# Starting the second stage of a two-stage kernel inside the first: normalized h transposed by DMA, weights loaded into freed buffers, and the first spatial block summed while z2 grows

## The chip, the cores and the metric

The kernel runs on one core of a Trainium2 chip. The metric is the time of one execution in device microseconds (us). Most executions of one kernel agree within 0.3%; medians of several runs are quoted. The trace of one profiled execution has a span that is about 2 us shorter than its timed run. A core has five engines with instruction streams of their own: PE (matrix multiply), ACT (activation functions), DVE (elementwise work and statistics), POOL and SP; SP issues the DMAs here. In the traces an engine works through its stream in the order in which it was written, and the streams wait for each other through semaphores.

## The reference, cut to what matters

```python
# stage one: attention over 64 segments of 32 rows, each with 8 memory rows from the segment before
h  = x + A_ref(layernorm(x), mem0, Wq, Wk, Wv, Wo)
# stage two: a gated unit with a mixing matrix over the sequence
def B_ref(x, w_in, w_sp, b_sp, w_out):
    z  = gelu(x @ w_in)                      # 2048 x 1792
    z1 = z[:, :896]
    z2 = layernorm(z[:, 896:])
    g  = w_sp @ z2 + b_sp[:, None]           # 2048 x 2048 times 2048 x 896: the "mixing"
    return (z1 * g) @ w_out
h2 = h + B_ref(layernorm(h), w_in, w_sp, b_sp, w_out)
```

Stage one is serial from segment to segment. Stage two needs h; a row block is 128 of the 2048 rows, so there are 16. The mixing needs all of z2, but a sum over its row blocks may start with the first. The mixing is done in four blocks of 512 outputs; the title and the recorded texts call such a block a spatial block.

## The kernel before: the parts that matter

The code runs through a helper that records each operation with what it reads and writes, and inserts the waits. `pe`, `act`, `dve`, `pool` and `sp` append to an engine's stream, so the order in the text is the order on each engine. Eight PSUM banks take the results of PE.

The end of stage one, and the loads of stage two (cut):

```python
    lastA = em.by_eng["pe"][-1]
    for qr in range(4):
        WoX_mm(RB - 1, qr)            # the last row block's leftover output projection
    WoX_evac(RB - 1)
    WoX_scatter(RB - 1, WXB)
    h_done(RB - 1, WXB)               # adds it to h, statistics of h, stores h to DRAM
    ...
    sp(lambda e: e.dma_start(w_in, winr), writes=["w_in"], after=[lastA])
    for rb in range(RB):
        sp(lambda e, rb=rb: e.dma_start(h_sb[:, rb, :], h_d[rb]), ..., after=[lastA])   # h is read back
    ...                               # w_out, bias
    load_wT(0)                        # w_sp, transposed earlier
    load_wT(1)
```

The loop over row blocks of z2, and the mixing:

```python
    for rb in range(2):
        xn_apply(rb); xT(rb % 2, 6 + rb % 2); xn_copy(rb, 6 + rb % 2)
    for rb in range(RB):
        if rb + 2 < RB:
            xn_apply(rb + 2)                     # DVE: normalize h of block rb+2
        z2_mm(rb, 0)                             # PE: 4 matmuls, then gelu on ACT
        if rb + 2 < RB:
            xT(rb % 2, 6 + rb % 2)               # PE: 4 transposes of block rb+2 into a bank
            xn_copy(rb + 2, 6 + rb % 2)          # DVE: bank to SBUF
        z2_mm(rb, 1)                             # PE: 4 matmuls, then gelu on ACT
        z2_norm(rb)                              # DVE: statistics of z2, wait for both gelus
        if rb > 0:
            z2_apply(rb - 1)                     # DVE: normalize z2
        if rb % 4 == 3:
            for fb in range(FB):
                z1_group(rb // 4, fb)            # PE: 7 groups of 4 matmuls, gelu on ACT
    z2_apply(RB - 1)
    check()                                      # overflow check: DVE, one tiny matmul, DVE
    for tb in range(NTB):                        # 4 blocks of 512 outputs
        for fb in range(FB):
            bank = fb % 2
            for sc in range(RB):                 # 16 mixing matmuls into one bank
                pe(... ps[:, bank, 0:TB], lhsT=z2[:, sc, ...], rhs=wTb[tb % 2][:, :, sc, :] ...)
            ...                                  # "gate": DVE adds the bias, multiplies by z1
            if pend and fb >= 1:
                out_rb(pend.pop(0))              # 7 output matmuls, adds h, stores
```

Of the kernel before, what the change touches and what calls it, by code (L numbers as in the profile page):

```python
# [6 lines left out]
BF = mybir.dt.bfloat16  # L7
# [153 lines left out]
def fast_path(nc, st, keep, A_x, A_mem0, A_Wq, A_Wk, A_Wv, A_Wo, A_seg_len, B_w_in, B_w_sp, B_b_sp, B_w_out, out):  # L161
# [15 lines left out]
    CK = 16  # L177
# [44 lines left out]
    hbuf = sb("hbuf", [128, 4, 512], BF)  # L222
    wst = sb("wst", [128, RB, 64], BF)
# [21 lines left out]
    vext_d = nc.dram_tensor("vext_d", [NCK, 16, 128, 2 * DH], BF, kind="Internal").ap()  # L245
    h_d = nc.dram_tensor("h_d", [RB, 128, D], BF, kind="Internal").ap()
# [396 lines left out]


# [82 lines left out]

    qx_copy(0)
    for s in range(NSEG):
# [17 lines left out]
        for b in range(2):  # L747
            for mi in range(2):
                QK(s, b, mi)
                QK_evac(s, b, mi)  # L750
        S_half(s, 0)
# [5 lines left out]
        S_half(s, 1)  # L757
        sm_exp(1)
        sm_rcp(0)
# [4 lines left out]
        V_half(s, 1, (2, 3))  # L764
        V_evac(1, "act")
        sm_norm(0)
        sm_norm(1)
        if s + 1 < NSEG:
            qx_copy(s + 1)
        ev = gx.pour(16)  # L770
# [25 lines left out]
        mem_out(s)  # L796
# [6 lines left out]
        if j4 == 3:  # L803
            F_group(rb, XB)
            F_add(rb, XB)
        if j4 == 3 and rb >= 1:
            WoX_scatter(rb - 1, WXB)
            h_done(rb - 1, WXB)
    assert not gx.atoms and not gv.atoms
    lastA = em.by_eng["pe"][-1]  # L810
    for qr in range(4):
        WoX_mm(RB - 1, qr)
    WoX_evac(RB - 1)
    WoX_scatter(RB - 1, WXB)
    h_done(RB - 1, WXB)
    endA = em.by_eng["pe"][-1]


    w_in = region(4 * WSZ, DC * F).rearrange("p (dc f) -> p dc f", dc=DC)
    xn2T = region(4 * WSZ + QX, DC * S).rearrange("p (dc t) -> p dc t", dc=DC)  # L820
    h_sb = region(0, RB * D).rearrange("p (rb d) -> p rb d", rb=RB)
    wTb = [region(RB * D, RB * 512).rearrange("p (t sc c) -> p t sc c", sc=RB, c=64),
           region(WSZ, RB * 512).rearrange("p (t sc c) -> p t sc c", sc=RB, c=64)]
    off = WSZ + RB * 512
    w_out = region(off, FB * D).rearrange("p (fb d) -> p fb d", fb=FB)
    off += FB * D
    bsp_b = region(off, S)
    off += S
    gt = region(off, 2 * 2 * 512).bitcast(F32).rearrange("p (j t) -> p j t", j=2)
    off += 2048  # L830
    assert off <= 2 * WSZ
    z2 = region(2 * WSZ, RB * FH).rearrange("p (rb f) -> p rb f", rb=RB)
    z1T = region(3 * WSZ, FB * S).rearrange("p (fb t) -> p fb t", fb=FB)
    TB = 512
    NTB = S // TB
    HF = FH // 2

    winr = B_w_in.rearrange("(dc p) f -> p dc f", p=128)
    sp(lambda e: e.dma_start(w_in, winr), writes=["w_in"], after=[lastA])
    for rb in range(RB):  # L840
        sp(lambda e, rb=rb: e.dma_start(h_sb[:, rb, :], h_d[rb]), reads=[("hd", rb)], writes=[("hs", rb)], after=[lastA])
    woutr = B_w_out.rearrange("(fb p) d -> p fb d", p=128)
    sp(lambda e: e.dma_start(w_out, woutr), writes=["w_out"], after=[lastA])
    sp(lambda e: e.dma_start(bsp_b, bass.AP(B_b_sp.tensor, B_b_sp.offset, [[0, 128], [1, S]])), writes=["bsp"], after=[lastA])
    em.mark_const("w_in", "w_out")

    def load_wT(tb):
        for t in range(8):
            sp(lambda e, t=t: e.dma_start(wTb[tb % 2][:, t, :, :], wT_d[8 * tb + t]), reads=[("wTd", 8 * tb + t)],
               writes=[("wT", tb % 2, t)], after=[lastA])  # L850

    load_wT(0)
    load_wT(1)


# [9 lines left out]
    def xn_apply(rb):  # L865
# [52 lines left out]
    for rb in range(2):  # L918
        xn_apply(rb)
        xT(rb % 2, 6 + rb % 2)  # L920
        xn_copy(rb, 6 + rb % 2)
# [814 lines left out]
```

## Time and profile before

The median is 1034.83 us (3 runs, 1034.33 to 1035.91); the span of the profiled run is 1032.3 us.

| part of the span | from, us | to, us | what PE does |
|---|---|---|---|
| stage one | 0 | 815.55 | to its last output-projection (Wo) matmul |
| hand-over | 815.55 | 832.57 | some 3 us of leftover matmuls that both kernels need, some small ones, waits |
| z2 loop | 832.57 | 902.93 | z2, z1 and transposes |
| mixing and output | 902.93 | 1032.3 | nearly full |

From the page of the profile, part 1 (busy us, share of the span, instructions by engine) and part 4 (the chain that ended last, by engine; PEld are PE's weight loads, SPq and ACTq the queues of SP and ACT, "issue" is time in which an engine waited for nothing that the profile shows):

```profile
PE 899.6 (87%) x18986; PEld 443.2 (43%) x18997; DVE 471.5 (46%) x1059; ACT 489.8 (47%) x1095; POOL 108.0 (10%) x276
PE 79%; ACT 12%; DVE 3%; SPq 2%; issue 2%; DMA 2%; POOL 0%; ACTq 0%
```

PE is the engine to win time on, and it is busy for 87% of the span. The timeline of PE at the hand-over (start, length, engine, line, operation, count; in brackets the idle time before it and what ended it; the first line holds the last Wo matmuls, and two small groups at 816.26 and 816.37 are left out):

```profile
813.64 1.91 PE L579 MATMUL f_ps<-f_arena,f_cT 128*32 128x512 bf16 x32
817.34 0.40 PE L631 MATMUL f_ps<-f_partx,f_Sc 128*32 128x512 bf16 x4 [0.58 <-ACT f_partx L626]
818.53 1.91 PE L621 MATMUL f_ps<-f_arena,f_cTx 128*32 128x512 bf16 x32 [0.80 <-DVE f_hbuf L611]
821.14 0.40 PE L631 MATMUL f_ps<-f_partx,f_Sc 128*32 128x512 bf16 x4 [0.70 <-ACT f_partx L626]
830.72 0.61 PE L346 MATMUL f_ps<-f_ident,f_xn 128*128 128x128 bf16 x4 [9.18 <-DVE f_xn L867]
832.17 0.61 PE L346 MATMUL f_ps<-f_ident,f_xn 128*128 128x128 bf16 x4 [0.84 <-DVE f_xn L867]
832.57 1.70 PE L878 MATMUL f_ps<-f_arena 128*128 128x448 bf16 x4
```

Leftover groups with waits between them, then 9.18 us of idle until the first block of h has come back and been normalized on DVE (the waits list gives that DVE operation 7.0 us of waiting for the DMA of h). The same four transposes take 0.61 us here and 0.40 us later: PE is on a slow clock. The windows view (here 831 to 838 us) gives the clock that PE was granted, after the busy times of the five engines:

```profile
831.00:838.00 7.00, 5.42 (x24) 2.51 (x21) 3.57 (x9) 1.63 (x3) 0.23 (x1) 0.59 1.11 354
```

0.59 of full speed. The Trainium skill, "TensorE: Matmul & The Clock Gate", Part 1, says that PE falls to half rate after an idle window of about 3.4 us and needs about as long of work to recover; the 9.18 us of idle and the 0.59 agree. Finer windows show a granted clock of 0.50 from 823.0 to 836.7 us: it fell 1.5 us after PE's last matmul, and came back 6.0 us after the first transposes.

The chain of waits inside the z2 loop (start, length, what):

```profile
852.98 0.77 PE f_ps L878 x4
853.75 0.02 issue
853.77 0.55 ACT f_arena L881
854.33 0.02 issue
854.35 0.64 DVE f_st L892
854.99 0.02 issue
855.01 0.21 DVE f_mv L894
855.22 0.38 DVE f_arena L903
855.60 0.34 DVE f_xn L867
855.93 0.05 issue
855.98 0.40 PE f_ps L346 x4
856.38 0.77 PE f_ps L878 x4
```

L878 is a z2 group, L881 its gelu, L892 and L894 the statistics of z2, L903 the normalization of the z2 block before, L867 the normalization of h for a later row block, L346 the transposes of that. One turn, from 852.98 to 856.38, is 3.40 us. L867 stands behind L892 in DVE's stream, and PE cannot pass the transposes that wait for L867. In all, PE waits 24.1 us for L867 before twelve groups of transposes.

### The profile page before, as it was taken

Reading aid. Unit: us, or ns where it says so; the run is one execution under the profiler, and the core shown is the slowest. Engines: PE = TensorE matmul, PEld = TensorE weight load, DVE = VectorE, ACT = ScalarE, POOL = GpSimd, SP = SyncE. Lnnn points to the kernel's source line nnn. Section 1 sums busy time; section 2 is a strip of 40 time slices with the busy share of each in tenths; the row PEclk is TensorE's granted clock in tenths of the full one; section 3 lists DMA queues with packets and bytes.
Section 4 is the critical chain, followed back from the end, with each engine's and each line's share of the span. In section 5 each row is a group of like instructions: output and inputs, shape, how many; then the busy total and the mean of one; then the engine's idle time right before and its main releaser. Section 6 shows DMA issues by size and latency. Waiting matters only on the chain.

```text
span 1032.3 us, 41294 instructions
## 1 busy us (share of the span) xinstructions
PE 899.6 (87%) x18986; PEld 443.2 (43%) x18997; DVE 471.5 (46%) x1059; ACT 489.8 (47%) x1095; POOL 108.0 (10%) x276
## 2 busy tenths in 40 slices
PE   5588999999999999899999998888888667899997
PEld 4444444444444444444444444333333223344443
DVE  2144455454455455454544444443444345533443
ACT  2155555665556555555655555655555434500000
POOL 4000001111001111010101000111000012200000
PEclk9889999999999999999999999999999979999999
DMA  9931122121121112112211112020201190002200
GB/s 334 353 73 34 46 45 54 49 57 44 34 49 34 49 39 55 36 47 45 60 48 37 46 44 64 8 65 8 62 13 45 32 352 1 1 8 96 97 16 32
DMA packets 93491, 67.34 MB, mean 65 GB/s; under 512 B 54392, under 2 KB 78336, under 8 KB 93312
## 3 DMA queue, kind: packets, MB, share of 16 engines
q1 hardware_dynamic: 93312, 64.65, 21.4%
q8 instruction: 150, 2.46, 1.0%
q14 instruction: 29, 0.24, 0.1%
HBM read 39.46 MB, written 16.78 MB: 54 GB/s over the span
## 4 chain that ended last, share of the span: by engine, by line
PE 79%; ACT 12%; DVE 3%; SPq 2%; issue 2%; DMA 2%; POOL 0%; ACTq 0%
PE f_ps L436 22%; PE f_ps L579 12%; PE f_ps L956 9%; PE f_ps L530 7%; PE f_ps L380 6%; PE f_ps L621 3%; ACT f_part L591 3%; PE f_ps L496 3%; ACT f_E_sb L489 3%; ACT f_R_sb L508 2%; PE f_ps L911 2%; PE f_ps L944 2%; PE f_ps L547 2%; PE f_ps L597 2%; PE f_ps L878 2%
## 5 line engine op out<-in xcount | busy, mean ns | idle before, releaser
L436 PE MATMUL f_ps<-f_arena,f_hT 128*32 128x512 bf16 x4096 | 233.4, 380 | 15.7 <-ACT f_hT L600 15.6
L443 ACT ACTIVATE f_Tst<-f_ps 128x512 bf16<-128x512 f32 x256 | 152.9, 597 | 112.9 <-PE f_ps L436 112.9
L436 PEld LDWEIGHTS f_ps<-f_arena,f_hT 128*32 128x32 bf16 x4096 | 105.2, 97 | 120.7 <-ACT f_hT L600 20.5
L530 PE MATMUL f_ps<-f_arena,f_hT 128*32 128x512 bf16 x2048 | 143.6, 378 | 0.0
L449 DVE STREAM_TRANSPOSE f_QT<-f_Tst 128x256 uint32<-128x256 uint32 x128 | 56.5, 442 | 188.0 <-ACT f_Tst L443 188.0
L579 PE MATMUL f_ps<-f_arena,f_cT 128*32 128x512 bf16 x2048 | 122.3, 380 | 2.2 <-ACT f_cT L566 2.2
L956 PE MATMUL f_ps<-f_arena 128*128 128x512 bf16 x448 | 99.3, 379 | 3.0 <-DVE f_arena L961 2.4
L591 ACT ACTIVATE f_part<-f_ps 128x512 bf16<-128x512 f32 x64 | 38.2, 597 | 108.0 <-PE f_ps L579 108.0
L452 DVE STREAM_TRANSPOSE f_KT<-f_Tst 128x256 uint32<-128x256 uint32 x128 | 57.0, 445 | 53.1 <-ACT f_Tst L443 53.1
L579 PEld LDWEIGHTS f_ps<-f_arena,f_cT 128*32 128x32 bf16 x2048 | 48.8, 96 | 74.0 <-ACT f_cT L566 32.3
L568 DVE TENSOR_SCALAR f_cT<-f_ps 128x320 bf16<-128x320 f32 x128 | 56.9, 487 | 33.0 <-PE f_ps L553 33.0
L459 POOL COPY f_QT<-f_arena 128x256 bf16<-128x256 bf16 x64 | 29.9, 467 | 397.9 <-PE f_ps L481 397.8
L380 PEld LDWEIGHTS f_ps<-f_hTe,f_arena 128*128 128x128 bf16 x1024 | 61.5, 102 | 20.7 <-issue 20.6
L380 PE MATMUL f_ps<-f_hTe,f_arena 128*128 128x128 bf16 x1024 | 70.1, 227 | 0.0
L956 PEld LDWEIGHTS f_ps<-f_arena 128*128 128x128 bf16 x448 | 43.5, 98 | 56.4 <-DVE f_arena L961 3.8
L516 DVE SCALAR_TENSOR_TENSOR f_E_sb<-f_R_sb,f_E_sb 128x160 bf16<-128x160 f32 x128 | 41.7, 326 | 54.6 <-ACT f_R_sb L512 54.6
L566 ACT ACTIVATE f_cT<-f_ps 128x320 bf16<-128x320 f32 x128 | 49.0, 434 | 37.1 <-PE f_ps L553 37.1
L489 ACT ACTIVATE f_E_sb<-f_ps,f_shift 128x224 bf16<-128x224 f32 x128 | 57.0, 445 | 0.0
L512 ACT ACTIVATE f_R_sb<-f_R_sb,f_rbias 128x160 f32<-128x160 f32 x128 | 54.0, 422 | 2.1
L508 ACT ACTIVATE f_R_sb<-f_ps 128x160 f32<-128x160 f32 x128 | 39.0, 304 | 29.8 <-PE f_ps L501 25.0
L961 DVE TENSOR_TENSOR f_arena<-f_ps,f_arena 128x512 f32<-128x512 f32 x28 | 19.4, 692 | 70.6 <-PE f_ps L956 70.6
L346 PE MATMUL f_ps<-f_ident,f_xn 128*128 128x128 bf16 x144 | 15.8, 238 | 39.3 <-DVE f_xn L867 24.1
(95 smaller groups left out, 1087.3 us busy)
## 6 DMA issues: line engine op xcount, KB each, us to landing
wT_d<-f_wst SPq DMA_DIRECT2D x32, 256.0 KB, 2.3
f_arena<-wT_d SPq DMA_DIRECT2D x32, 256.0 KB, 7.6
f_arena<-in_A_Wq_dram SPq DMA_DIRECT2D x4, 1024.0 KB, 10.5
f_arena<-in_A_Wk_dram SPq DMA_DIRECT2D x4, 1024.0 KB, 14.0
f_arena<-in_A_Wv_dram SPq DMA_DIRECT2D x4, 1024.0 KB, 13.1
f_arena<-in_A_Wo_dram SPq DMA_DIRECT2D x4, 1024.0 KB, 13.9
vext_d<-f_Vs SPq DMA_DIRECT2D x32, 128.0 KB, 2.0
f_Vx<-vext_d SPq DMA_DIRECT2D x64, 64.0 KB, 2.6
```

The source lines that it names most:

```text
L380: pe(lambda e, h=h, dc=dc, hh=hh: e.matmul(ps[:, bank, hh * 128:(hh + 1) * 128], lhsT=ws[:, dc, h * DH:(h + 1) * DH], rhs=hTe[:, ck % 2, d ...
L436: pe(lambda e, dc=dc, c=c, rhs=rhs: e.matmul(ps[32 * c:32 * c + 32, bank, :], lhsT=hT[:, sl, dc, :], rhs=rhs, start=(dc == 0), stop=(dc == ...
L443: act(lambda e: e.activation(out=Tst[:, tb, :].rearrange("p (hp i r) -> p hp i r", i=32, r=2), in_=ps[:, bank, :].rearrange("p (hp r i) -> ...
L449: dve(lambda e: e.transpose(out=dst, in_=src), reads=[("T", tb)], writes=[("QT", b)])
L452: dve(lambda e: e.transpose(out=dst, in_=src), reads=[("T", tb)], writes=[("KT", b)])
L489: act(lambda e: e.activation(out=E_sb[:, b, :], in_=ps[:, bank, 0:224], func=ACT.Exp, scale=scale, bias=shift_sb[:, 0:1]), reads=[PB(bank) ...
L508: act(lambda e: e.activation(out=R_sb[:, b, :], in_=ps[:, bank, 224:384], func=ACT.Ln, scale=LNS), reads=[PB(bank)], writes=[("R", b)])
L530: pe(lambda e, dc=dc, c=c, c0=c0: e.matmul(ps[32 * c:32 * c + 32, bank, :], lhsT=hT[:, sl, dc, :], rhs=w_v[:, dc, c0:c0 + 512], start=(dc ...
L568: dve(lambda e: e.tensor_scalar(out=dst, in0=src, scalar1=UNSC, scalar2=None, op0=ALU.mult), reads=[PB(PVB[c])], writes=[("cT", c)])
L579: pe(lambda e, h=h, g=g, i=i, k=k, b=b: e.matmul(ps[32 * g:32 * g + 32, OB, :], lhsT=cTh[:, i, 8:40], rhs=w_o[:, h, :], start=(first and k ...
L591: act(lambda e: e.activation(out=part[:, s % 4, :], in_=ps[:, OB, :], func=ACT.Copy), reads=[PB(OB)], writes=[("part", s % 4)])
L956: pe(lambda e, fb=fb, sc=sc, bank=bank, tb=tb: e.matmul(ps[:, bank, 0:TB], lhsT=z2[:, sc, fb * 128:(fb + 1) * 128], rhs=wTb[tb % 2][:, :, ...
```

## The change: its intent and its diff

The intent is to start stage two before stage one has ended, and to leave PE no waits in the z2 loop:

1. h is normalized on DVE inside stage one (`xn2_apply`), stored, and transposed by DMA into the freed half of a buffer; only the last two of 16 row blocks are still transposed on PE.
2. w_in, the first w_sp block and the bias are loaded into freed buffers before stage one ends. The first z2 group stands directly behind the last Wo matmul; the leftover projection follows it.
3. z1 groups go two at a time between the row blocks of z2, and the mixing of the first block of outputs, for five of seven column groups in five banks of their own, runs along four row blocks behind z2. z2 and z1 then take turns in three banks, where they had two each.

The diff also leaves out the memory rows of the last segment, which no segment reads (16 small matmuls, L597 of the kernel before).

The diff, cut to its core:

```diff
+    def xn2_apply(rb, j):
+        dve(lambda e: e.tensor_scalar(out=xo[:, j, :], in0=hbuf[:, rb % 4, :], scalar1=mv[:, rb, 0:1], ...
+    def xn2T_dma(rb, after):
+        sp(lambda e: e.dma_start_transpose(out=xts[rb // 8][:, rb % 8, :, :], in_=xn2_d[rb]), ...
 ...                                      # in the loop over the 64 segments of stage one:
+        if s == NSEG - 1:
+            load_wT(0, [lastop["q"]])
 ...
+        if s == NSEG - 1:
+            sp(... w_in1 ..., after=[lastop["s"], lastop["x"]])
+            sp(... bsp_b ..., after=[lastop["k"]])
+            for r in range(8, RB - 2):
+                xn2T_dma(r, [lastop["s"], lastop["x"]])
 ...
+        if j4 == 0 and rb >= 2:
+            xn2_apply(rb - 2, rb % 2)
+            xn2_store(rb - 2, rb % 2)
+        if s == 3 * CK:
+            sp(... w_in2 ..., after=free0)
+        if 0 <= s - 3 * CK - 1 < 8:
+            xn2T_dma(s - 3 * CK - 1, free0)
 ...                                      # stage two:
+    LAG = 4
     for rb in range(RB):
-        if rb + 2 < RB:
-            xn_apply(rb + 2)
-        z2_mm(rb, 0)
-        if rb + 2 < RB:
-            xT(rb % 2, 6 + rb % 2)
-            xn_copy(rb + 2, 6 + rb % 2)
-        z2_mm(rb, 1)
+        z2_mm(rb, 0, zbank())             # three banks in turn for z2 and z1
+        if rb == 0:
+            ...                           # leftovers of row blocks 14 and 15
+        z2_mm(rb, 1, zbank())
+        if rb == 0:
+            for qr in range(4):
+                WoX_mm(RB - 1, qr)
+        ...                               # leftovers, PE transposes of blocks 14 and 15
         z2_norm(rb)
         if rb > 0:
             z2_apply(rb - 1)
-        if rb % 4 == 3:
-            for fb in range(FB):
-                z1_group(rb // 4, fb)
+        for _ in range(2):
+            if rb >= 1 and z1list and (z1list[0][0] < 3 or rb >= 12):
+                tb, fb = z1list.pop(0)
+                z1_group(tb, fb, zbank())
+        if rb >= LAG:
+            for fb, bk in enumerate(ACC):
+                mix(0, fb, rb - LAG, bk)
     z2_apply(RB - 1)
-    check()
 ...                                      # rest of the first block's mixing, then, after that block:
+        if tb == 0:
+            check()
```

More of the change, by code (lines that the diff above doesn't have):

```diff
@@ L222, in fast_path @@
     hbuf = sb("hbuf", [128, 4, 512], BF)
+    xo = sb("xo", [128, 2, 512], BF)
     wst = sb("wst", [128, RB, 64], BF)
@@ L245, in fast_path @@
     vext_d = nc.dram_tensor("vext_d", [NCK, 16, 128, 2 * DH], BF, kind="Internal").ap()
+    xn2_d = nc.dram_tensor("xn2_d", [RB, 128, D], BF, kind="Internal").ap()
     h_d = nc.dram_tensor("h_d", [RB, 128, D], BF, kind="Internal").ap()
@@ L642, in h_done, with xn2_store @@
         sp(lambda e: e.dma_start(h_d[rb], hbuf[:, rb % 4, :]), reads=[("h", rb % 4)], writes=[("hd", rb)])
+    def xn2_apply(rb, j):
+        dve(lambda e: e.tensor_scalar(out=xo[:, j, :], in0=hbuf[:, rb % 4, :], scalar1=mv[:, rb, 0:1], scalar2=rstd[:, rb:rb + 1],
+                                      op0=ALU.subtract, op1=ALU.mult),
+            reads=[("h", rb % 4), ("mv", rb), ("rstd", rb)], writes=[("xo", j)])
+    def xn2_store(rb, j):
+        sp(lambda e: e.dma_start(xn2_d[rb], xo[:, j, :]), reads=[("xo", j)], writes=[("xn2d", rb)])
+    WH = DC * FH
+    w_in2 = region(4 * WSZ, WH).rearrange("p (dc f) -> p dc f", dc=DC)
+    w_in1 = region(4 * WSZ + QX, WH).rearrange("p (dc f) -> p dc f", dc=DC)
+    xts = [region(4 * WSZ + i * QX + WH, 8 * D).rearrange("p (r dc t) -> p r dc t", r=8, dc=DC) for i in range(2)]
+    winr = B_w_in.rearrange("(dc p) f -> p dc f", p=128)
+    def xn2T_dma(rb, after):
+        sp(lambda e: e.dma_start_transpose(out=xts[rb // 8][:, rb % 8, :, :], in_=xn2_d[rb]), reads=[("xn2d", rb)], writes=[("xn2T", rb)],
+           after=after)
     NWT = S // 64
@@ L726, in fast_path, with load_wT @@
     VXN = [2] * 12 + [4, 4, 0, 0]
+    wTb = [region(0, RB * 512).rearrange("p (t sc c) -> p t sc c", sc=RB, c=64),
+           region(3 * WSZ, RB * 512).rearrange("p (t sc c) -> p t sc c", sc=RB, c=64)]
+    h_sb = region(RB * 512, RB * D).rearrange("p (rb d) -> p rb d", rb=RB)
+    z1T = region(WSZ, FB * S).rearrange("p (fb t) -> p fb t", fb=FB)
+    bsp_b = region(WSZ + FB * S, S)
+    z2 = region(2 * WSZ, RB * FH).rearrange("p (rb f) -> p rb f", rb=RB)
+    gt = region(2 * WSZ + RB * FH, 2048).bitcast(F32).rearrange("p (j t) -> p j t", j=2)
+    w_out = region(3 * WSZ + RB * 512, FB * D).rearrange("p (fb d) -> p fb d", fb=FB)
+    def load_wT(tb, after):
+        for t in range(8):
+            sp(lambda e, t=t: e.dma_start(wTb[tb % 2][:, t, :, :], wT_d[8 * tb + t]), reads=[("wTd", 8 * tb + t)],
+               writes=[("wT", tb % 2, t)], after=after)
+    lastop = {}
     qx_copy(0)
@@ L749, in fast_path @@
                 QK(s, b, mi)
+                lastop["qk"[mi]] = em.by_eng["pe"][-1]
                 QK_evac(s, b, mi)
+        if s == NSEG - 1:
+            load_wT(0, [lastop["q"]])
         S_half(s, 0)
@@ L757, in fast_path @@
         S_half(s, 1)
+        lastop["s"] = em.by_eng["pe"][-1]
         sm_exp(1)
+        if s == NSEG - 1:
+            sp(lambda e: e.dma_start(w_in1, winr[:, :, 0:FH]), writes=["w_in1"], after=[lastop["s"], lastop["x"]])
+            sp(lambda e: e.dma_start(bsp_b, bass.AP(B_b_sp.tensor, B_b_sp.offset, [[0, 128], [1, S]])), writes=["bsp"], after=[lastop["k"]])
+            for r in range(8, RB - 2):
+                xn2T_dma(r, [lastop["s"], lastop["x"]])
         sm_rcp(0)
@@ L764, in fast_path @@
         V_half(s, 1, (2, 3))
+        lastop["v"] = em.by_eng["pe"][-1]
         V_evac(1, "act")
@@ L769, in fast_path @@
             qx_copy(s + 1)
+            lastop["x"] = em.by_eng["pool"][-1]
+            lastop["x"] = em.by_eng["pool"][-1]
         ev = gx.pour(16)
@@ L795, in fast_path @@
             late.append(lambda: xe_copy(ck + 1, XB))
-        mem_out(s)
+        if s + 1 < NSEG:
+            mem_out(s)
         for f in late:
@@ L802, in fast_path @@
             load_vx(s + 2)
-        if j4 == 3:
+        if j4 == 3 and s + 1 < NSEG:
             F_group(rb, XB)
             F_add(rb, XB)
-        if j4 == 3 and rb >= 1:
-            WoX_scatter(rb - 1, WXB)
-            h_done(rb - 1, WXB)
-    assert not gx.atoms and not gv.atoms
-    lastA = em.by_eng["pe"][-1]
-    for qr in range(4):
-        WoX_mm(RB - 1, qr)
-    WoX_evac(RB - 1)
-    WoX_scatter(RB - 1, WXB)
-    h_done(RB - 1, WXB)
-    endA = em.by_eng["pe"][-1]
-    w_in = region(4 * WSZ, DC * F).rearrange("p (dc f) -> p dc f", dc=DC)
-    xn2T = region(4 * WSZ + QX, DC * S).rearrange("p (dc t) -> p dc t", dc=DC)
-    h_sb = region(0, RB * D).rearrange("p (rb d) -> p rb d", rb=RB)
-    wTb = [region(RB * D, RB * 512).rearrange("p (t sc c) -> p t sc c", sc=RB, c=64),
-           region(WSZ, RB * 512).rearrange("p (t sc c) -> p t sc c", sc=RB, c=64)]
-    off = WSZ + RB * 512
-    w_out = region(off, FB * D).rearrange("p (fb d) -> p fb d", fb=FB)
-    off += FB * D
-    bsp_b = region(off, S)
-    off += S
-    gt = region(off, 2 * 2 * 512).bitcast(F32).rearrange("p (j t) -> p j t", j=2)
-    off += 2048
-    assert off <= 2 * WSZ
-    z2 = region(2 * WSZ, RB * FH).rearrange("p (rb f) -> p rb f", rb=RB)
-    z1T = region(3 * WSZ, FB * S).rearrange("p (fb t) -> p fb t", fb=FB)
+            if rb >= 1:
+                WoX_scatter(rb - 1, WXB)
+                h_done(rb - 1, WXB)
+        if j4 == 0 and rb >= 2:
+            xn2_apply(rb - 2, rb % 2)
+            xn2_store(rb - 2, rb % 2)
+        if s == 3 * CK:
+            free0 = [done47["s"], done47["x"]]
+            sp(lambda e: e.dma_start(w_in2, winr[:, :, FH:F]), writes=["w_in2"], after=free0)
+        if 0 <= s - 3 * CK - 1 < 8:
+            xn2T_dma(s - 3 * CK - 1, free0)
+        if s == 3 * CK - 1:
+            done47 = {"s": lastop["s"], "x": px}
+        px = lastop.get("x")
+    assert not gx.atoms and not gv.atoms
+    lastQ, lastK, lastV = lastop["q"], lastop["k"], lastop["v"]
     TB = 512
@@ L836, in fast_path, with xT2 @@
     HF = FH // 2
-    winr = B_w_in.rearrange("(dc p) f -> p dc f", p=128)
-    sp(lambda e: e.dma_start(w_in, winr), writes=["w_in"], after=[lastA])
-    for rb in range(RB):
-        sp(lambda e, rb=rb: e.dma_start(h_sb[:, rb, :], h_d[rb]), reads=[("hd", rb)], writes=[("hs", rb)], after=[lastA])
-    woutr = B_w_out.rearrange("(fb p) d -> p fb d", p=128)
-    sp(lambda e: e.dma_start(w_out, woutr), writes=["w_out"], after=[lastA])
-    sp(lambda e: e.dma_start(bsp_b, bass.AP(B_b_sp.tensor, B_b_sp.offset, [[0, 128], [1, S]])), writes=["bsp"], after=[lastA])
-    em.mark_const("w_in", "w_out")
-    def load_wT(tb):
-        for t in range(8):
-            sp(lambda e, t=t: e.dma_start(wTb[tb % 2][:, t, :, :], wT_d[8 * tb + t]), reads=[("wTd", 8 * tb + t)],
-               writes=[("wT", tb % 2, t)], after=[lastA])
-    load_wT(0)
-    load_wT(1)
+    em.mark_const("w_in1", "w_in2", "w_out")
+    def xT2(rb):
+        return xts[rb // 8][:, rb % 8, :, :]
     def check():
@@ L863, in check, with xn_copy, z2_mm @@
             reads=[PB(5)], writes=["flag"])
-    def xn_apply(rb):
-        j = rb % 2
-        dve(lambda e: e.tensor_scalar(out=xn[:, j, :], in0=h_sb[:, rb, :], scalar1=mv[:, rb, 0:1], scalar2=rstd[:, rb:rb + 1],
-                                      op0=ALU.subtract, op1=ALU.mult),
-            reads=[("hs", rb), ("mv", rb), ("rstd", rb)], writes=[("xn", j)])
-    def xn_copy(rb, bank):
+    def xn_copy(rb, j, bank):
         src = psb[:, bank, 0:512].rearrange("p (dc c) -> p dc c", dc=DC)
-        dve(lambda e: e.tensor_copy(out=xn2T[:, :, rb * 128:(rb + 1) * 128], in_=src), reads=[PB(bank)], writes=[("xn2T", rb)], after=[lastA])
-    def z2_mm(rb, hf):
-        bank = 2 + hf
+        dve(lambda e: e.tensor_copy(out=xT2(rb), in_=src), reads=[PB(bank)], writes=[("xn2T", rb)], after=[lastop["s"], lastop["x"]])
+    def z2_mm(rb, hf, bank):
         for dc in range(DC):
-            pe(lambda e, dc=dc: e.matmul(ps[:, bank, 0:HF], lhsT=xn2T[:, dc, rb * 128:(rb + 1) * 128],
-                                         rhs=w_in[:, dc, FH + hf * HF:FH + (hf + 1) * HF], start=(dc == 0), stop=(dc == DC - 1)),
-               reads=["w_in", ("xn2T", rb)], writes=[PB(bank)])
+            pe(lambda e, dc=dc: e.matmul(ps[:, bank, 0:HF], lhsT=xT2(rb)[:, dc, :], rhs=w_in2[:, dc, hf * HF:(hf + 1) * HF],
+                                         start=(dc == 0), stop=(dc == DC - 1)),
+               reads=["w_in2", ("xn2T", rb)], writes=[PB(bank)])
         act(lambda e: e.activation(out=z2[:, rb, hf * HF:(hf + 1) * HF], in_=ps[:, bank, 0:HF], func=ACT.Gelu_apprx_tanh),
-            reads=[PB(bank)], writes=[("z2", rb, hf)], after=[lastA])
-    mvz = stats
+            reads=[PB(bank)], writes=[("z2", rb, hf)], after=[lastV])
     st2 = sb("st2", [128, 2, 2, 6], F32)
@@ L905, in z2_apply, with z1_group @@
             reads=[("z2", rb, 0), ("z2", rb, 1), ("mv2", j), ("rs2", j)], writes=[("z2", rb, 0), ("z2", rb, 1)])
-    def z1_group(tb, fb):
-        bank = fb % 2
-        rd_x = [("xn2T", r) for r in range(4 * tb, 4 * tb + 4)]
+    def z1_group(tb, fb, bank):
+        r0 = 4 * tb
         for dc in range(DC):
-            pe(lambda e, dc=dc: e.matmul(ps[:, bank, 0:TB], lhsT=w_in[:, dc, fb * 128:(fb + 1) * 128],
-                                         rhs=xn2T[:, dc, tb * TB:(tb + 1) * TB], start=(dc == 0), stop=(dc == DC - 1)),
-               reads=["w_in"] + rd_x, writes=[PB(bank)])
+            pe(lambda e, dc=dc: e.matmul(ps[:, bank, 0:TB], lhsT=w_in1[:, dc, fb * 128:(fb + 1) * 128],
+                                         rhs=xts[r0 // 8][:, r0 % 8:r0 % 8 + 4, dc, :], start=(dc == 0), stop=(dc == DC - 1)),
+               reads=["w_in1"] + [("xn2T", r) for r in range(r0, r0 + 4)], writes=[PB(bank)])
@@ L914, in z1_group, with mix @@
         act(lambda e: e.activation(out=z1T[:, fb, tb * TB:(tb + 1) * TB], in_=ps[:, bank, 0:TB], func=ACT.Gelu_apprx_tanh),
-            reads=[PB(bank)], writes=[("z1T", fb, tb)], after=[endA])
+            reads=[PB(bank)], writes=[("z1T", fb, tb)], after=[lastK])
+    def mix(tb, fb, sc, bank):
+        pe(lambda e: e.matmul(ps[:, bank, 0:TB], lhsT=z2[:, sc, fb * 128:(fb + 1) * 128], rhs=wTb[tb % 2][:, :, sc, :],
+                              start=(sc == 0), stop=(sc == RB - 1)),
+           reads=[("z2", sc, 0), ("z2", sc, 1)] + [("wT", tb % 2, t) for t in range(8)], writes=[PB(bank)])
@@ new lines, in gate, with zbank @@
+    def gate(tb, fb, bank):
+        tsl = slice(tb * TB, (tb + 1) * TB)
+        dve(lambda e: e.tensor_tensor(out=gt[:, fb % 2, :], in0=ps[:, bank, 0:TB], in1=bsp_b[:, tsl], op=ALU.add),
+            reads=[PB(bank), "bsp"], writes=[("gt", fb % 2)], after=[lastV])
+        dve(lambda e: e.tensor_tensor(out=z1T[:, fb, tsl], in0=gt[:, fb % 2, :], in1=z1T[:, fb, tsl], op=ALU.mult),
+            reads=[("gt", fb % 2), ("z1T", fb, tb)], writes=[("z1T", fb, tb)])
+    zcnt = [0]
+    def zbank():
+        zcnt[0] += 1
+        return 5 + zcnt[0] % 3
@@ L917, in fast_path @@
     act(lambda e: e.preload_act_table_set("gelu_apprx_tanh_and_others"))
-    for rb in range(2):
-        xn_apply(rb)
-        xT(rb % 2, 6 + rb % 2)
-        xn_copy(rb, 6 + rb % 2)
+    z1list = [(tb, fb) for tb in range(NTB) for fb in range(FB)]
+    ACC = (0, 1, 2, 3, 4)
+    LAG = 4
     for rb in range(RB):
-        if rb + 2 < RB:
-            xn_apply(rb + 2)
-        z2_mm(rb, 0)
-        if rb + 2 < RB:
-            xT(rb % 2, 6 + rb % 2)
-            xn_copy(rb + 2, 6 + rb % 2)
-        z2_mm(rb, 1)
+        z2_mm(rb, 0, zbank())
+        if rb == 0:
+            WoX_scatter(RB - 2, 1)
+            F_group(RB - 1, XB)
+            h_done(RB - 2, 1)
+            F_add(RB - 1, XB)
+        z2_mm(rb, 1, zbank())
+        if rb == 0:
+            for qr in range(4):
+                WoX_mm(RB - 1, qr)
+            endA = em.by_eng["pe"][-1]
+            WoX_evac(RB - 1)
+            load_wT(1, [endA])
+            sp(lambda e: e.dma_start(w_out, B_w_out.rearrange("(fb p) d -> p fb d", p=128)), writes=["w_out"], after=[endA])
+        if rb == 1:
+            WoX_scatter(RB - 1, 1)
+            h_done(RB - 1, 1)
+            for r in range(RB):
+                sp(lambda e, r=r: e.dma_start(h_sb[:, r, :], h_d[r]), reads=[("hd", r)], writes=[("hs", r)], after=[lastQ])
+        if rb in (1, 2):
+            xn2_apply(RB - 3 + rb, rb % 2)
+        if rb in (2, 3):
+            r, j, bank = RB - 4 + rb, (rb - 1) % 2, zbank()
+            for dc in range(DC):
+                pe(lambda e, dc=dc, j=j, bank=bank: e.transpose(out=psb[:, bank, dc * 128:(dc + 1) * 128], in_=xo[:, j, dc * 128:(dc + 1) * 128],
+                                                                identity=ident[:, :]), reads=[("xo", j), "ident"], writes=[PB(bank)])
+            xn_copy(r, j, bank)
@@ L932, in fast_path @@
             z2_apply(rb - 1)
-        if rb % 4 == 3:
-            for fb in range(FB):
-                z1_group(rb // 4, fb)
-    z2_apply(RB - 1)
-    check()
+        for _ in range(2):
[5 more added lines that the diff above has]
+                mix(0, fb, rb - LAG, bk)
+    z2_apply(RB - 1)
+    while z1list:
+        tb, fb = z1list.pop(0)
+        z1_group(tb, fb, zbank())
+    for fb, bk in enumerate(ACC):
+        for sc in range(RB - LAG, RB):
+            mix(0, fb, sc, bk)
+        gate(0, fb, bk)
     outr = out[0].rearrange("(rb p) d -> p rb d", p=128)
@@ L952, in fast_path @@
     for tb in range(NTB):
-        for fb in range(FB):
-            bank = fb % 2
+        for fb in range(len(ACC) if tb == 0 else 0, FB):
+            bank = 5 + fb % 3 if tb == 0 else fb % 2
             for sc in range(RB):
-                pe(lambda e, fb=fb, sc=sc, bank=bank, tb=tb: e.matmul(
-                    ps[:, bank, 0:TB], lhsT=z2[:, sc, fb * 128:(fb + 1) * 128], rhs=wTb[tb % 2][:, :, sc, :],
-                    start=(sc == 0), stop=(sc == RB - 1)),
-                    reads=[("z2", sc, 0), ("z2", sc, 1)] + [("wT", tb % 2, t) for t in range(8)], writes=[PB(bank)])
-            tsl = slice(tb * TB, (tb + 1) * TB)
-            dve(lambda e, fb=fb, bank=bank, tsl=tsl: e.tensor_tensor(out=gt[:, fb % 2, :], in0=ps[:, bank, 0:TB], in1=bsp_b[:, tsl], op=ALU.add),
-                reads=[PB(bank), "bsp"], writes=[("gt", fb % 2)])
-            dve(lambda e, fb=fb, tsl=tsl: e.tensor_tensor(out=z1T[:, fb, tsl], in0=gt[:, fb % 2, :], in1=z1T[:, fb, tsl], op=ALU.mult),
-                reads=[("gt", fb % 2), ("z1T", fb, tb)], writes=[("z1T", fb, tb)])
+                mix(tb, fb, sc, bank)
+            gate(tb, fb, bank)
             if pend and fb >= 1:
                 out_rb(pend.pop(0))
+        if tb == 0:
+            check()
         pend.extend(range(4 * tb, 4 * tb + 4))
         if tb + 2 < NTB:
-            load_wT(tb + 2)
+            load_wT(tb + 2, [])
     for rb in pend:
```

## The prediction

> **What bounds it.** PE, in both stages (first page: PE busy 87% of a 1032.3 us span; the chain that ended last is 79% PE). Stage one (attention, to 815.6 us, its last Wo matmul in the timeline) is hardly touched. Stage two shows three losses in the chain of waits and the timeline:
> 1. The hand-over. From 815.55 to 832.57, where the first z2 group starts, PE does only about 5 us of matmuls. The rest is evictions, the store of h, and a 9.2 us PE idle until h is read back (DMA link 7.07 us), then normalizing and transposing.
> 2. Cold PE. After that idle the first two z2 groups took 1.49 and 1.51 us, later ones 0.77; granted clock 0.59 from 831 to 838. The Trainium skill ("TensorE: Matmul & The Clock Gate", Part 1) says an idle window of about 3.4 us drops PE to half rate; this trace agrees.
> 3. The z2 loop. Each row block pays matmul, gelu (0.55), statistics (0.64), normalize, transpose in series: period 3.40 us for 1.9 us of PE work. From 832.57 to 902.93, where mixing starts, PE issues only 24.4 us of z2 (128 x 0.19), 24.3 of z1 (112 x 0.2165) and 5 of transposes.
>
> From 902.93 to the end PE is nearly full (448 mixing and 112 output matmuls at 0.2165 = 121.3 of 129.4 us).
>
> **What the change does.** It normalizes h inside stage one (14 DVE operations of 0.40 us, where DVE waits 4.46 us for ACT), stores it and transposes 14 blocks by DMA (a similar transpose now lands in about 3.5 us), off the chain. w_in, the first w_sp block and the bias load before stage one ends. 56 of 64 PE transposes go. z1 groups and 80 mixing matmuls of the first block fill the z2 loop's waits; PE then has 3.3 us (later 4.4) of work per row block against ACT 2.3 and DVE 1.9, so PE should bound it.
>
> **Sum.** From 815.6: z2 24.4, z1 24.3, mixing 97.0, output 24.2, leftover projection, gather and scatters 3.2, eight transposes 0.9: 174.0, so 989.6. Stalls: waiting for partx at the hand-over 0.5; the last z2 block's normalization 0.7; the overflow check, now between mixing blocks, waits for two DVE gates of 0.69 and small operations: 2; bank-0 gate at two block boundaries 1.5; last gate and tail as now, 1.4 + 5.1. Span about 1001; a timed run is 2.5 above the span. Slop 0.5: **1003 us, 998 to 1010** (ratio 0.97). Chances: faster by over 2% 0.93, within 2% 0.06, slower 0.01. All of the 32 us is on the chain: about 12 from hand-over and cold clock, 20 from the z2 loop.
>
> **What would show it.** First z2 matmul within 0.5 us of the last Wo matmul; no PE idle over 3 us between 800 and 880, granted clock near 1.0 there; z1 never waiting on w_in by more than 1 us; row blocks 4 to 11 about 4.4 us apart; last z2 group near 867; first mixing group of block two near 885, after a PE wait of about 2 us at the check; stage one unchanged within 1 us; PE busy above 89%.
>
> **What would make it wrong.** (a) Data late: w_sp (2.1 MB), half of w_in and the bias (1.4 MB) are issued only from about 808; at the present reload's 350 to 390 GB/s they land near 818 to 820, z1 needs them at 822; slow transposes in the SP queue would delay more. (b) Three banks rotating among z2 and z1: if ACT falls behind, PE waits. (c) SP's in-order waits delaying stage one's V loads. (d) DVE backlog in row blocks 0 to 2, with h's residual additions in front of the normalization. Each costs a few us, not the gain.

## The result, and the profile after

The changed kernel takes 999.64 us (4 runs, 999.08 to 999.91) against 1034.76 us (4 runs): a ratio of 0.9658, 95% interval 0.9642 to 0.9675. A ratio here is the mean time of one kernel's runs over that of the other's of the same rounds, so it is not quite the ratio of the medians. The span of the profiled run is 997.6 us, 34.7 us less.

The same two lines of the page:

```profile
PE 891.6 (89%) x18918; PEld 441.2 (44%) x18925; DVE 465.8 (47%) x1045; ACT 489.2 (49%) x1094; POOL 107.9 (11%) x276
PE 81%; ACT 12%; SPq 2%; issue 2%; DMA 1%; DVE 1%; POOL 0%; ACTq 0%
```

PE's timeline at the hand-over:

```profile
812.94 1.91 PE L581 MATMUL f_ps<-f_arena,f_cT 128*32 128x512 bf16 x32
814.78 0.93 PE L897 MATMUL f_ps<-f_arena 128*128 128x448 bf16 x4
816.04 0.40 PE L633 MATMUL f_ps<-f_partx,f_Sc 128*32 128x512 bf16 x4 [0.33 <-ACT f_partx L628]
```

The first z2 group (L897) stands on the last Wo matmuls (L581) without a gap, at full speed, and the granted clock is 1.00 in every window from 816 to 920 us. The chain of waits inside the loop has only PE in it; one turn of z2 (L897), two z1 groups (L928) and five mixing matmuls (L935) is 4.32 us, all work:

```profile
834.39 1.51 PE f_ps L897 x8
835.90 1.73 PE f_ps L928 x8
837.63 1.08 PE f_ps L935 x5
838.71 1.51 PE f_ps L897 x8
```

From the waits list, what PE still waits for between 800 us and the end (total us, times, longest), without those that belong to stage one:

```profile
PE f_ps L886 <- DVE f_okb L885: 1.8, 1, 1.8
PE f_ps L935 <- DVE f_arena L941: 1.6, 2, 0.8
PE f_ps L935 <- DVE f_arena L921: 0.6, 1, 0.6
PE f_ps L633 <- ACT f_partx L628: 0.3, 1, 0.3
```

Two short ones are left out here: 0.3 us of issue behind the check and 0.2 us for the last gate. The four are the overflow check (L886), the gate of a bank that the next block of outputs wants at once (L941), the last row block's normalization (L921) and the hand-over (L633).

Where the 34.7 us of the span come from, by marks that both timelines have:

| stretch | before | after | saved |
|---|---|---|---|
| start to last Wo matmul | 815.55 | 814.85 | 0.70 |
| from there to the first mixing matmul of the second block of outputs (before at 928.06, after at 894.39) | 112.51 | 79.54 | 32.97 |
| from there to the end | 104.24 | 103.21 | 1.03 |

The lines at the second mark, before and after:

```profile
928.06 1.25 PE L956 MATMUL f_ps<-f_arena 128*128 128x512 bf16 x5 [0.79 <-DVE f_arena L961]
894.39 7.07 PE L935 MATMUL f_ps<-f_arena 128*128 128x512 bf16 x32 [0.26 <-issue]
```

The 0.70 us are not an effect that is shown: over the profiles of all runs the last Wo matmul ends between 813.75 and 815.55 us, with no order by kernel.

### The profile page after: what moved, and what is told of

Its sections match the earlier page's. It is cut to its first block, busy times and chain, and to the rows that moved or that the text cites. A ratio compares the mean times of both kernels' runs of the same rounds, so it can differ in the third digit from the quotient of the medians. Undisturbed runs are those within 1.5% of the kernel's fastest.

```text
span 997.6 us, 41195 instructions
## 1 busy us (share of the span) xinstructions
PE 891.6 (89%) x18918; PEld 441.2 (44%) x18925; DVE 465.8 (47%) x1045; ACT 489.2 (49%) x1094; POOL 107.9 (11%) x276
## 4 chain that ended last, share of the span: by engine, by line
PE 81%; ACT 12%; SPq 2%; issue 2%; DMA 1%; DVE 1%; POOL 0%; ACTq 0%
PE f_ps L438 23%; PE f_ps L581 12%; PE f_ps L935 10%; PE f_ps L532 8%; PE f_ps L382 6%; PE f_ps L623 3%; ACT f_part L593 3%; PE f_ps L498 3%; ACT f_E_sb L491 3%; ACT f_R_sb L510 2%; PE f_ps L897 2%; PE f_ps L928 2%; PE f_ps L1008 2%; PE f_ps L549 2%; PE f_ps L599 2%
## 5 line engine op out<-in xcount | busy, mean ns | idle before, releaser
L581 PE MATMUL f_ps<-f_arena,f_cT 128*32 128x512 bf16 x2048 | 122.3, 380 | 2.3 <-ACT f_cT L568 2.2
L935 PE MATMUL f_ps<-f_arena 128*128 128x512 bf16 x448 | 101.3, 379 | 2.4 <-DVE f_arena L941 1.6
L581 PEld LDWEIGHTS f_ps<-f_arena,f_cT 128*32 128x32 bf16 x2048 | 48.8, 96 | 74.0 <-ACT f_cT L568 32.2
L935 PEld LDWEIGHTS f_ps<-f_arena 128*128 128x128 bf16 x448 | 43.5, 98 | 55.9 <-DVE f_arena L941 2.6
L589 POOL COPY f_cTx<-f_cT 128x256 bf16<-128x256 bf16 x64 | 26.1, 408 | 212.5 <-DVE f_cT L570 212.5
L401 PE MATMUL f_ps<-f_arena,f_hTe 128*32 128x512 bf16 x512 | 38.6, 411 | 9.1 <-ACT f_Vs L408 9.1
## 6 DMA issues: line engine op xcount, KB each, us to landing
f_arena<-in_A_Wk_dram SPq DMA_DIRECT2D x4, 1024.0 KB, 13.9
```

Source lines behind the costliest of these rows:

```text
L581: pe(lambda e, h=h, g=g, i=i, k=k, b=b: e.matmul(ps[32 * g:32 * g + 32, OB, :], lhsT=cTh[:, i, 8:40], rhs=w_o[:, h, :], start=(first and k ...
L935: pe(lambda e: e.matmul(ps[:, bank, 0:TB], lhsT=z2[:, sc, fb * 128:(fb + 1) * 128], rhs=wTb[tb % 2][:, :, sc, :], start=(sc == 0), stop=(s ...
```

## The experiments

Ten runs were made, two of them repeats; all gave correct results. The kernel before was run beside them; its median was 1034.12, 1034.16 and 1034.15 us, from 7, 9 and 10 runs (the 10 are the 9 and one more).

| run | median us | against the kernel before (95%) | what it is |
|---|---|---|---|
| the change | 999.64 | 0.9658 (0.9642 to 0.9675) | |
| after_again | 999.21 | 0.9666 (0.9654 to 0.9678) | the change, run again |
| a_nomix | 999.52 | 0.9670 (0.9654 to 0.9686) | the change without early mixing |
| a_nofill | 1000.36 | 0.9672 (0.9655 to 0.9688) | the change without early mixing and without interleaved z1 |
| a_nofill_2 | 999.71 | 0.9668 (0.9654 to 0.9681) | the same, run again |
| a_late | 1007.39 | 0.9739 (0.9724 to 0.9754) | the change with all loads and DMA transposes after stage one |
| a_late_nofill | 1007.49 | 0.9744 (0.9731 to 0.9757) | both |
| b_fill | 1022.16 | 0.9885 (0.9869 to 0.9902) | the kernel before with interleaved z1 |
| b_lagnorm | 1028.61 | 0.9951 (0.9935 to 0.9968) | the kernel before with z2's statistics one block later on DVE |
| b_warm | 1032.12 | 0.9979 (0.9966 to 0.9993) | the kernel before with useless matmuls in the idle stretch |
| a_best | 994.49 | 0.9616 (0.9603 to 0.9629) | the change with its remaining waits removed |

The prediction's reading was that the fillers, z1 groups and early mixing matmuls, take up the waits of the z2 loop; that is theory B of the first two experiments. The rival, theory A, says that the waits came from the order of DVE's and PE's streams, through the transposes; once these have left the loop nothing in it holds PE, and the order of PE's work is indifferent.

### a_nomix: without the early mixing

```diff
-    LAG = 4
+    LAG = RB
```

> The changed kernel, but the first spatial block is no longer summed while z2 grows: its 80 early mixing matmuls come after the loop over row blocks; z1 groups stay interleaved. Theory A (once the transposes have left the loop, nothing in it holds PE, so the order of PE's work is indifferent): 999 us, within 1 us of the changed kernel, possibly 0.6 us faster because the wait for the last row block's normalization is covered. Theory B (the prediction's: the mixing fills waits of the z2 loop, 0.2165 us for each of 80 matmuls): up to 17 us slower, about 1010 to 1017 us.

Measured: 999.52 us against 999.64. Moving 80 mixing matmuls out of the loop changes nothing that the runs can show. In its trace, the wait of 0.6 us for the last normalization is gone, as expected. Theory B falls for the mixing.

### a_nofill and a_nofill_2: without either filler

```diff
-    LAG = 4
+    LAG = RB
 ...
-        for _ in range(2):
-            if rb >= 1 and z1list and (z1list[0][0] < 3 or rb >= 12):
+        for _ in range(FB if rb % 4 == 3 else 0):
+            if True:
```

> The changed kernel with neither filler: z1 groups run in blocks of seven after every fourth row block, as before the change, and all mixing after the loop; h is still normalized, stored and transposed by DMA in stage one. Theory A (the transposes and their copies leaving the loop is what removed the waits): row blocks 1.5 us apart in PE, no waits over 0.5 us except at the first three blocks, where DVE is late with the residual additions; 999 to 1002 us. Theory B (the waits are gelu, statistics and normalization latency, and only filling removes them): row blocks 2 to 3 us apart, 1008 to 1020 us.

> The version without either filler, repeated beside the changed kernel because the two differed by less than the noise of their separate calls. Theory A (filler is worth nothing once h arrives transposed): within 1 us of the changed kernel of this call; its trace shows 0.9 us of waits at two transposes less 0.6 us at the last normalization. Theory B: 8 us or more slower.

Measured: 1000.36 us, and 999.71 us beside 999.21 us for the change. Of the change's 35 us, the two fillers together give about half a microsecond, within the spread of the runs. The traces say the same with less scatter. From the last Wo matmul to the last matmul of all takes 178.71 us in the change (178.72 in after_again), 177.93 in a_nomix and 179.21 in a_nofill_2. It takes 180.90 in a_nofill, but there the granted clock was 0.50 for 3.4 us after the wait of 1.80 us at the check: 32 mixing matmuls took 8.75 us in place of 7.07. PE's timeline of a_nofill:

```profile
824.62 0.40 PE L981 MATMUL f_ps<-f_ident,f_xo 128*128 128x128 bf16 x4 [0.43 <-DVE f_arena L893]
824.85 6.27 PE L928 MATMUL f_ps<-f_arena 128*128 128x512 bf16 x28
830.96 6.22 PE L897 MATMUL f_ps<-f_arena 128*128 128x448 bf16 x32
837.01 6.21 PE L928 MATMUL f_ps<-f_arena 128*128 128x512 bf16 x28
```

32 z2 matmuls, four row blocks, run in 6.05 us (830.96 to 837.01), 1.51 us a block, with nothing between them. In the kernel before, a block took 3.40 us. The only waits left in the loop are at the two row blocks that are still transposed on PE (0.44 us at 822.28 and the 0.43 us above). z2's statistics and normalization run behind on DVE, and PE needs them only for the mixing. The three banks came with the change too and no run tests them alone; but in the old loop PE never waited for a bank: between 833 and 903 us its waits are 14.1 us for L867 and 0.6 us for the last gelu.

### b_fill: the kernel before with interleaved z1

```diff
-        if rb % 4 == 3:
-            for fb in range(FB):
-                z1_group(rb // 4, fb)
+        for _ in range(2):
+            if z1list and rb >= 4 * z1list[0][0] + 1:
+                z1_group(*z1list.pop(0))
+    while z1list:
+        z1_group(*z1list.pop(0))
```

> The kernel before, with one part of the change alone: up to two z1 groups after each row block in place of seven after every fourth. Hand-over and PE transposes stay. Theory A says that the wait in the old loop is the chain gelu, statistics, normalize, transpose of 2.3 us in DVE's order, and two z1 groups (1.73 us) plus half a z2 pair (0.77 us) cover it: period 3.4 to 3.6 us including the z1 work, loop about 11 us shorter, 1022 to 1026 us. If filler does not cover the wait (ACT or the banks bound it): 1031 to 1035 us.

Measured: 1022.16 us, 12.0 us less than the kernel before. Where two z1 groups stand behind a row block, the transposes no longer wait:

```profile
841.55 0.39 PE L346 MATMUL f_ps<-f_ident,f_xn 128*128 128x128 bf16 x4
841.77 0.92 PE L878 MATMUL f_ps<-f_arena 128*128 128x448 bf16 x4
842.53 1.89 PE L911 MATMUL f_ps<-f_arena 128*128 128x512 bf16 x8
844.25 0.92 PE L878 MATMUL f_ps<-f_arena 128*128 128x448 bf16 x4
845.01 0.39 PE L346 MATMUL f_ps<-f_ident,f_xn 128*128 128x128 bf16 x4
```

The turn is 3.46 us, now with z1 in it. So filler is worth 12 us where the wait exists and nothing where it has been removed. The two are substitutes and do not add.

### b_lagnorm: the kernel before with z2's statistics one block later

```diff
         z2_mm(rb, 1)
-        z2_norm(rb)
         if rb > 0:
-            z2_apply(rb - 1)
+            z2_norm(rb - 1)
+        if rb > 1:
+            z2_apply(rb - 2)
 ...
+    z2_norm(RB - 1)
+    z2_apply(RB - 2)
     z2_apply(RB - 1)
```

> The kernel before, with the statistics and the normalization of a z2 row block issued one row block later on DVE, nothing else. Theory A (the 3.40 us period comes from DVE's order: the normalized h and its transpose for the block after next stand behind statistics that wait for the newest gelu): period falls to about 2.8 us, DVE's own work, in about 11 blocks, so 1028 to 1030 us. Rival (PE, ACT and bank latency set the period): 1034 to 1035 us.

Measured: 1028.61 us, 5.5 us less, by reordering DVE's stream alone. Its chain of waits:

```profile
852.78 0.41 PE f_ps L346 x4
853.20 0.02 issue
853.22 0.43 DVE f_arena L873
853.64 1.07 DVE f_st L892 x2
854.71 0.02 issue
854.74 0.21 DVE f_mv L894
854.95 0.38 DVE f_arena L903
855.32 0.33 DVE f_xn L867
855.66 0.05 issue
855.70 0.41 PE f_ps L346 x4
```

The gelu on ACT and the z2 group have left the chain; a turn is 2.92 us (852.78 to 855.70), DVE's own work and one transpose. This shows that the 3.40 us were set by the order on DVE, and that DVE's own work (normalizing, copying, statistics) then sets the turn of the old loop.

### a_late and a_late_nofill: the early loads and transposes undone

```diff
-        if s == NSEG - 1:
-            load_wT(0, [lastop["q"]])
 ...                        # likewise w_in, bias and all DMA transposes inside stage one
     assert not gx.atoms and not gv.atoms
+    late = [em.by_eng["pe"][-1], lastop["x"]]
+    sp(... w_in2 ..., after=late)
+    for r in range(2):
+        xn2T_dma(r, late)
+    sp(... w_in1 ..., after=late)
+    for r in range(2, 8):
+        xn2T_dma(r, late)
+    load_wT(0, late)
+    sp(... bsp_b ..., after=late)
+    for r in range(8, RB - 2):
+        xn2T_dma(r, late)
```

> The changed kernel, with the loads of w_in, of the first spatial block and of the bias and the 14 DMA transposes issued only after stage one's last output projection, in the order in which stage two needs them; the normalization and store of h stay inside stage one. This is the hand-over's early start undone. Theory: PE idles 7 to 9 us until half of w_in and the first transposed block have landed, then runs the first 3 us at half clock; 1009 to 1013 us, 10 to 13 us slower than the changed kernel. If transposes issued at 1.9 us each feed the row blocks too slowly, more: up to 1018 us. Rival (early start worth little because the z2 loop is what the change shortened): within 4 us of the changed kernel.

> Both undone: loads and DMA transposes only after stage one, and no filler. If filler is worth nothing whatever else holds: 1007 to 1008 us, as with the late loads alone. If filler is worth something when the transposed blocks are late (each transpose occupies its issuing queue for about 1.5 us, as long as a row block of z2 alone takes PE, against 3.2 us with two z1 groups): 1009 to 1014 us, with PE waits for transposed blocks in the first eight row blocks.

Measured: 1007.39 us, 7.8 us more than the change's 999.64 of the earlier call (8.2 more than after_again, which ran on the same chip), and 1007.49 us without filler, 8.3 us more than the change of that call. The expectation of 10 to 13 us was too high; its alternative of under 4 us is further off. PE's timeline of a_late, the first z2 group:

```profile
820.60 1.68 PE L893 MATMUL f_ps<-f_arena 128*128 128x448 bf16 x4 [5.54 <-DMA f_arena<-xn_d]
```

The wait is 5.54 us, not 7 to 9, and PE is cold after it (four z2 matmuls in 1.68 us against 0.93; the first five groups are 2.4 us longer in sum than in the change). The wait and the slow start make up the difference. The wait names a transposed block (from xn_d); the run undoes loads and transposes together, so what each is worth alone is not known. In a_late_nofill it was possible that late transposes, each issued in 1.2 to 1.5 us, would hold up row blocks that take 1.51 us. They did not: that trace shows no wait for a transposed block after the first. Filler was worth nothing there either.

### b_warm: useless matmuls in the idle stretch of the kernel before

```diff
     endA = em.by_eng["pe"][-1]
+    for _ in range(40):
+        pe(lambda e: e.matmul(ps[:, 5, :], lhsT=ident[:, :], rhs=hTe[:, 0, :, :], start=True, stop=True), ...
```

> The kernel before, with 40 matmuls of no use on a free bank in the 9.2 us in which PE waits for h to be read back. Theory: PE keeps its clock, the first two z2 groups take 0.77 us in place of 1.49 and 1.51 us, granted clock 1.0 after 831 us; 1032 to 1033 us, about 2 us faster. Rival (those groups wait for w_in or h, not for the clock): no change, and the groups stay at 1.5 us.

Measured: 1032.12 us, 2.0 us less (0.7 to 3.5 us by the interval). The windows view, 831 to 838 us, for comparison with 0.59 before:

```profile
831.00:838.00 7.00, 5.01 (x35) 2.60 (x36) 4.52 (x11) 2.00 (x4) 0.83 (x2) 1.00 1.11 350
```

From the first transposes to the first mixing matmul it takes 70.37 us (831.00 to 901.37) against 72.21 us (830.72 to 902.93): the cold clock cost 1.84 us. The first z2 group starts no earlier, so this is the clock alone. In this profile an earlier group, the leftover projection, ran at half speed (3.52 us against 1.91): the granted clock was 0.50 from 817.1 to 820.5 us, though no wait of PE just before was longer than 0.80 us. Of the other profiles only a_nofill's has such a fall without a long idle, and why it comes is not known. This is why the stretch is the better measure than the span.

### a_best: the change with its remaining waits removed

```diff
-    LAG = 4
+    LAG = RB
 ...                        # check() split: its DVE part at rb == 4, its matmul into free bank 0 at rb == 8
+        if rb == 4:
+            check_dve()
+        if rb == 8:
+            check_pe()
 ...
-            bank = 5 + fb % 3 if tb == 0 else fb % 2
+            bank = 5 + fb % 3 if tb == 0 else (fb + tb) % 2
 ...
-        if tb == 0:
-            check()
```

> The changed kernel itself, unaltered, as the yardstick on this chip for the next three runs. 999 to 1000 us.

> The changed kernel without early mixing and with its three remaining PE waits in stage two taken away: the overflow check moved into the z2 loop on a free bank (1.8 us of wait and about 0.4 us around it), the mixing banks swapped from one block of outputs to the next (two waits of 0.79 us), and the last normalization covered (0.6 us). Theory (each of these waits is on the chain, one for one): 995 to 996 us, 4 to 4.5 us faster than the changed kernel. Rival (they hide other waits, such as DVE's gates): less than 2 us faster.

Measured: 994.49 us (993.51 to 995.11), 4.7 us less than the change (999.21). What PE waits for in stage two is now down to:

```profile
PE f_ps L633 <- ACT f_partx L628: 0.3, 1, 0.3
PE f_ps L1014 <- DVE f_arena L945: 0.2, 1, 0.2
```

The waits that were taken away add up to 4.0 us (1.8, 1.6 and 0.6), 4.4 with the tiny matmul and the restart around the check (893.97 to 894.39). Within the spread of the runs they came off the time one for one. This version beats both kernels.

## Why the prediction was right or wrong

The prediction was right in the time: 1003 us, range 998 to 1010, measured 999.64. Point by point:

- **Hand-over.** Right. The first z2 group starts on the last Wo matmul, no idle over 3 us, clock 1.00, z1 never waits for w_in. The size, "about 12 from hand-over and cold clock", was too small. Before, 17.02 us passed between last Wo and first z2; after, the leftovers that PE must do anyway take 2.8 us by the chain (0.40, 0.21, 1.84 and 0.33) and the one wait 0.33 us. That leaves 13.9 us, and the cold clock was measured at 1.84 us: between 15 and 16. Undoing the early loads and transposes gives back 7.8 to 8.3 us of it. The rest must come from what those runs kept: h is not read back, and the leftovers stand behind z2. That last step is a difference of two traces, not an experiment.
- **The z2 loop.** The size, "20 from the z2 loop", was right, the reason was not; to that extent the number was luck. The sum adds up PE's work and takes the waits as gone, whatever removes them, so its being right says nothing for the fillers. The step that failed: "z1 groups and 80 mixing matmuls of the first block fill the z2 loop's waits". Without both fillers the change is as fast (a_nofill_2 999.71, after_again 999.21). What removed the waits was that normalization, transposes and copies of h left the loop, and with them the only way by which DVE's order reached PE. b_lagnorm shows that this order set the 3.40 us; that the transposes were its way to PE is read from the chain, since no run puts them alone back into the new loop. The prediction's own line, "matmul, gelu, statistics, normalize, transpose in series", named the chain but not that half of its links were there by order only. Had it asked what PE would still wait for without the transposes, the answer, only ACT freeing a bank, was in the diff. By subtraction the loop itself gave about 19 us: 32.97 less 13.9 and 1.84, plus the 2.2 us that the moved check costs, less one bank wait of 0.79 that the new order avoids. In the trace before, 14.1 us of it are PE's waits for L867. About 2.6 us more are no wait but the PE time of twelve groups of transposes, 0.22 us each, which filler cannot save; the rest is not split further.
- **Stalls.** The check: predicted 2, measured 1.8 and 0.4 around it. Bank at two block boundaries: 1.5, measured 1.6. Last normalization: 0.7, measured 0.6. Hand-over: 0.5, measured 0.33.
- **The 3.4 us that were too many.** The last gate and the tail were put at 6.5 us. In the new trace the last matmul ends 4.0 us before the end of the span, and the last gate's wait is 0.22 us, most of it hidden by output matmuls that were ready; the trace before had the same 0.22 us, so 1.4 was too much for it there already. Those two account for 2.2 us. Stage one ended 0.7 us earlier in this profile, the timed run is 2.0 us above its span and not 2.5, and the slop of 0.5 was not needed; against that, the terms of the sum add up to 1003.8, not 1003.
- **Two marks contradicted the prediction's own sum.** It placed the last z2 group near 867 and the second block's first mixing near 885. They are at 876.55 and 894.39, within 2 us of where the sum itself (815.6 and the work and stalls listed) puts them. Only the marks were wrong.
- **Risks.** None happened. Six DMA transposes at the hand-over held SP for 11.34 us and landed after 6.2 us (median), slower than the 3.5 us assumed, but their row blocks came later. Row blocks 4 to 11 are 4.32 us apart (predicted about 4.4) except one with a single z1 group. PE is busy 89%.

## What to carry to other kernels

When PE waits in a loop, walk the chain and ask of each link whether the data need it or only the order of a stream does; a link by order can be removed by reordering or by moving the work out, and here filling the gap was then superfluous. Two remedies for one wait do not add: b_fill gained 12 us in the old loop and the same filler nothing in the new one. After such a change read the waits list again, for the small waits that are left may come off one for one: removing three kinds of them gave 4.7 us here.

## What the Trainium skill lacked or had wrong

- "TensorE: Matmul & The Clock Gate", Back-to-back issue gap: it gives about 131 ns per matmul as the sustained spacing at N = 512, against 216 ns from its formula for the isolated gap. Here 112 mixing matmuls, each with its own weights, back to back, took 24.36 us, 217.5 ns each; the formula fits this stream within 1%, and the 131 ns are not reached.
- The same page, Part 1, was right about the cold clock (granted clock 0.59 after 9.18 us of idle), but it ties the fall to an idle window of about 3.4 us. Two profiles show a clock of 0.50 for 3.4 us after shorter gaps: b_warm after waits of at most 0.80 us, a_nofill after one of 1.80 us, with PE busy for 1.4 of the last 3.4 us before. Other profiles have the same waits and no fall. The page works out the cost of such idles for a kernel that pays one at every tile, not for a single one; here one cost 1.84 us, measured by keeping PE busy with useless matmuls.
- "DMA: Bandwidth & Descriptors", Rules for kernel authors, advises to issue a DMA early and wait late; here that was worth 7.8 to 8.3 us. The page has a time in the issuing queue only for transposes of small tiles, in its part on trn3, and none for a DMA transpose of 128x512 on this chip; here it was 1.2 to 2.3 us (single ones in stage one; 11.34 us for six in a row), where most plain loads took about 0.5 us.
- "Perfetto Trace Analysis", Optimization Strategy, says to interleave regimes with different limits, and to find what each gap on the limiting engine waits for and make those dependencies start sooner or finish faster. That section does not say that the first can be superfluous once the second is done (b_fill 12.0 us in the old loop, both fillers about 0.5 us in the new one), nor that a dependency may exist by the order of another engine's stream alone; here that order was worth 5.5 us by itself (b_lagnorm).
